# Twenty steps of the weights' conversion in the attention, with a second wx buffer

## The chip, the cores and the metric

One core of a Trainium2 chip runs the whole program. The metric is the device time of one execution in microseconds; three timed runs of the kernel before gave 793.96, 794.51 and 795.60, median 794.51.

The engines are named as in the profile: PE is TensorE (PEld its weight loads), DVE is VectorE, ACT is ScalarE, POOL is GpSimd, SP is SyncE, which issues nearly all DMAs here. Each engine works through its own queue in order.

## The reference

Attention over 2 batches, 8 heads, 768 tokens and 64 dimensions, in which a query sees only the keys of its own cluster, and then two MLPs on the 1536 x 512 result. The weights come as float64.

```python
q_assign = np.argmax(np.einsum('bhsd,hcd->bhsc', q_n, c_n), axis=-1)
k_assign = np.argmax(np.einsum('bhsd,hcd->bhsc', k_n, c_n), axis=-1)
mask = q_assign[:, :, :, None] == k_assign[:, :, None, :]
scores = np.where(mask, scale * np.matmul(q, k.transpose(0, 1, 3, 2)), -1e9)
attn = softmax(scores)
x = (attn @ v).transpose(0, 2, 1, 3).reshape(1536, 512)
h = x @ moe_w_in                    # 512 x 2048
x = (h * np.cos(h)) @ moe_w_out     # 2048 x 512
h = x @ moe2_w_in
g = np.where(h >= 1, h, np.where(h <= -1, 0, (h + 1) ** 2 / 4))
out = g @ moe2_w_out
```

## The kernel before, in words

**Two parts of each number.** Products are made nearly exact by splitting a float32 into a high part hi, rounded to PE's short float32, and the rest lo. A product is then three matmuls: hi by hi, hi by lo, lo by hi (`mm3`, L749 to L751).

**The attention** goes through eight pairs of heads (two batches by four). A pair has four units (two heads by two halves of the queries), a unit six slots, so there are 32 units and 192 slots, 24 to a pair. `run_slot` (L664) emits one slot: the transposes of one key tile of the current unit (L569, the probabilities p of three query tiles), two score matmuls for tiles eight slots ahead (L517, L520), and products with v from slots four to eight of the unit (L594, L599, L600). In even slots come plo of two key tiles (L584, on DVE) and one exponential (L535, on ACT); in odd slots one row maximum (L526, on DVE). ACT copies each transposed tile out of PSUM (L572 or L577, phi), then DVE makes plo of it; the tiles' three PSUM banks (pool `ps_t`) are shared with the preparation. Scores have two buffers; the exponential frees one. The transposes that open a unit need the exponential issued two slots before.

While one pair runs, the next is prepared by `prep_pair`, a generator with one step per slot, started in slots 8, 32, 56, 80, 104 and 128. It transposes q and k (L349), makes th and tl on POOL (L321, L322), copies them into st by DMA (L335), assigns clusters, and in its 22nd step makes the parts of v (vv, L481, L482), loads the next v (L231, L232) and copies the one-hot rows oht by eight DMAs (L312). For the pair that is started in slot 80, this is slot 101.

Slots 18 to 179 lie in a manual schedule: PE, ACT, DVE and POOL keep the order of emission there. SP's queue, and everything outside, is ordered by the planner.

**The weights' conversion.** Each chunk is 128 x 2 x 512 of float64, read as pairs of 32-bit words. `issue_chunk` (L130) loads one into the single buffer wraw; `convert_chunk` (L138) turns it into hi and lo in six steps, between yields: abs (L145, ACT), clip (L147, DVE), shift (L149, DVE), or-low (L152, DVE), then or-high (L155, DVE) with hi (L161, POOL) and the issue of the next load, then lo (L164, DVE). Four chunks make the weights of one quarter: chunks 0 and 1 the first input weights, 2 and 3 the first output weights (moe_w_out). All steps run in one sequence, `weight_steps`; `pump(n)` takes n steps. One step is pumped in each of 16 slots of the attention, at the slot's end (slot % 8 == 5 from 69 to 189): chunks 0 and 1 whole, and chunk 2 up to or-low. In the MLP each output tile pumps one step, and `weight` (L194) pumps whatever is still missing before a weight is used.

**The MLPs** go through two layers, four quarters of the hidden dimension and three blocks of 512 tokens: `hidden` makes four tiles of h and their nonlinearity, `output` four tiles of the partial result y, one block behind. So the first two calls of `hidden` come before the first `output`, which reads chunks 2 and 3. Their hi and lo go into a buffer w_1 that exists only once the attention's pool is given up.

Of the kernel before, what the change touches and what calls it, by code (L numbers as in the profile page):

```python
# [1 line left out]

# [6 lines left out]
F32 = mybir.dt.float32  # L9
F32R = mybir.dt.float32r  # L10
# [8 lines left out]
P = 128  # L19
# [4 lines left out]
HIGH_MIN = 2.0 ** -15  # L24
HIGH_MAX = 122876.0
CHUNK = 6
P_BUFS = 6
NF = 2
NDVE = 2
# [4 lines left out]
def attention_moe_moe(  # L34
# [25 lines left out]
    HS = S // 2  # L60
# [51 lines left out]
    def next_slot():  # L112
        now[0] += 1
        for f, args in due.pop(now[0], ()):
            f(*args)
# [9 lines left out]
    w0pool = ctx.enter_context(tc.tile_pool(name="w0pool", bufs=1))  # L125
    wslot = []
    wchunks = []
    wraw = {}

    def issue_chunk(n):  # L130
        if n >= len(wchunks):
            return
        src, c0, _ = wchunks[n]
        raw = w0pool.tile([P, 2, 512], I64, tag="wraw", bufs=1, name=f"wraw{n}")
        nc.sync.dma_start(raw, src[:, c0:c0 + 2])
        wraw[n] = raw

    def convert_chunk(n):  # L138

        _, c0, w = wchunks[n]  # L140
        words = wraw.pop(n).bitcast(I32).rearrange("p c (f t) -> p c f t", t=2)
        low, high = words[:, :, :, 0], words[:, :, :, 1]
        x = w0pool.tile([P, 2, 512], F32, tag="wx", bufs=1, name=f"wx{n}")
        xi = x.bitcast(I32)
        nc.scalar.activation(x, high.bitcast(F32), AF.Abs)  # L145
        yield
        nc.vector.tensor_scalar(x, x, HIGH_MIN, HIGH_MAX, ALU.max, ALU.min)  # L147
        yield
        nc.vector.tensor_scalar(xi, xi, 3, 0x3FFFFFFF,  # L149
                                ALU.logical_shift_left, ALU.bitwise_and)  # L150
        yield
        nc.vector.scalar_tensor_tensor(xi, low, 29, xi,  # L152
                                       ALU.logical_shift_right, ALU.bitwise_or)
        yield
        nc.vector.scalar_tensor_tensor(xi, high, -0x40000000, xi,  # L155
                                       ALU.bitwise_and, ALU.bitwise_or)
        if not wslot:
            wslot.append(w0pool.tile([P, 2, 4, 512], F32R, tag="w_0", name="w_0"))
        t = wslot[w % 4]
        hi, lo = t[:, 0, c0:c0 + 2], t[:, 1, c0:c0 + 2]  # L160
        nc.gpsimd.tensor_scalar(hi, x, 1.0, 0.0, ALU.mult, ALU.add)  # L161
        issue_chunk(n + 1)
        yield
        nc.vector.tensor_tensor(lo, x, hi.bitcast(F32), ALU.subtract)  # L164
        yield
# [7 lines left out]
                                    (l * NQ + qi) * 2 + s))  # L173

    def weight_steps():
        for n in range(len(wchunks)):
            for _ in convert_chunk(n):
                yield n

    wsteps = weight_steps()  # L180

    def pump(n):

        for _ in range(n):
            at[0] += 1
            next(wsteps, None)
# [3 lines left out]
    def weight(l, qi, s):  # L190
        pump(2 * CHUNK * ((l * NQ + qi) * 2 + s + 1) - at[0])
        t = wslot[((l * NQ + qi) * 2 + s) % len(wslot)]
        return t[:, 0], t[:, 1]


    with ExitStack() as actx:
        ap = actx.enter_context(tc.tile_pool(name="apool", bufs=1))
# [308 lines left out]
        def scores(n, step):  # L506

            i, h, hf = units[n // HJ]
            j = hf * HJ + n % HJ
            qt, kt = prepped[i][1][h]  # L510
            if step == 0:
                ptile[n] = ps_s.tile([P, 2, 512], F32, tag="s", name=f"s{n}")
            s = ptile[n]
            cols = slice(j * P, (j + 1) * P)
            kc = slice(step * HS, (step + 1) * HS)
            with tc.issue_after(last_po[0]) if n == 0 and step == 0 else ExitStack():
                nc.tensor.matmul(s[:, step, :HS], qt[:, 0, cols], kt[:, 0, kc],  # L517
                                 start=True, stop=False)
            rows = D + C if i else D + 2 * C
            nc.tensor.matmul(s[:, step, :HS], qt[:rows, 1, cols], kt[:rows, 1, kc],  # L520
                             start=False, stop=True)

        def row_max(n):
            nm = ap.tile([P, 1], F32, tag="nm", bufs=8, name=f"nm{n}")
            s = ptile[n]
            nc.vector.tensor_reduce(nm, s[:, :, :HS], AX.XY, ALU.max, negate=True)  # L526
            ptile[n] = (s, nm)

        def row_exp(n):
            s, nm = ptile[n]  # L530
            u, jj = divmod(n, HJ)
            if jj == 0:
                dens[u] = ap.tile([P, HJ, 2], F32, tag="den", bufs=4, name=f"den{u}")
            p = ap.tile([P, 2, HS], F32, tag="p", bufs=P_BUFS, name=f"p{n}")
            nc.scalar.activation(p, s[:, :, :HS], AF.Exp, bias=nm,  # L535
                                 accum_out=dens[u][:, jj, 0:1])
            ptile[n] = p
            if jj == HJ - 1:
                later(2, inverse, u)
# [25 lines left out]
        def p_transpose(u, kt):  # L565
            ps = ps_t.tile([P, HS], F32, tag="t", name=f"pt{u}_{kt}")
            for jj in range(HJ):
                p = ptile[u * HJ + jj].rearrange("p a n -> p (a n)")
                nc.tensor.transpose(ps[:, jj * P:(jj + 1) * P], p[:, kt * P:(kt + 1) * P], ident)  # L569
            if kt < NF:  # L570
                pt = ap.tile([P, HS], F32, tag="phi", bufs=6, name=f"p{u}_t{kt}")
                nc.scalar.activation(pt, ps, AF.Copy)  # L572
                pts[(u, kt)] = pt
                return
            hi = ap.tile([P, HS], F32R, tag="phi", bufs=6, name=f"phi{u}_{kt}")
            lo = ap.tile([P, HS], F32R, tag="plo", bufs=5, name=f"plo{u}_{kt}")
            nc.scalar.activation(hi, ps, AF.Copy)  # L577
            pts[(u, kt)] = (hi, lo, ps)

        def p_lo(u, kt):  # L580
            if kt < NF:
                return
            hi, lo, ps = pts[(u, kt)]
            nc.vector.tensor_tensor(lo, ps, hi.bitcast(F32), ALU.subtract)  # L584

        def p_v(u, kt):
            i, h, hf = units[u]
            vv, v32 = prepped[i][0]
            if kt == 0:
                opsum[u] = ps_o.tile([P, HS], F32, tag="o", name=f"o{u}")  # L590
            o = opsum[u]
            if kt < NF:
                rows = slice(kt % 2 * D, (kt % 2 + 1) * D)
                nc.tensor.matmul(o[rows], v32[:, h, kt], pts.pop((u, kt)),  # L594
                                 start=(kt < 2), stop=False)
                return
            hi, lo, _ = pts.pop((u, kt))
            lhs = vv[:, kt - NF, h * P:(h + 1) * P]
            nc.tensor.matmul(o, lhs, hi, start=False, stop=False)  # L599
            nc.tensor.matmul(o, lhs, lo, start=False, stop=(kt == NJ - 1))  # L600
            if kt == NJ - 1:
                later(1, o_parts, u)
# [39 lines left out]


        LEAD, PREP, PREP1 = 8, 16, -8
        PV_AT = (4, 4, 5, 6, 7, 8)
        NSLOT = len(units) * NJ
        PAIR = 4 * NJ
# [10 lines left out]
        for u in range(len(units)):  # L658
            for kt in range(NJ):
                pv_slots.setdefault(u * NJ + PV_AT[kt], []).append((u, kt))  # L660
        preps = []
        prep_at = {(i - 1) * PAIR - PREP: i for i in range(2, len(pairs))}
        prep_at[PREP1] = 1
        def run_slot(slot):  # L664
            g = slot + LEAD
            if slot in prep_at:
                preps.append(prep_pair(prep_at[slot]))
            if 0 <= slot < NSLOT:
                p_transpose(slot // NJ, slot % NJ)
            if 0 <= g < NSLOT:  # L670
                scores(g // 2, g % 2)
            for u, kt in pv_slots.get(slot, ()):
                p_v(u, kt)
            if slot % 2 == 0:
                for s in (slot - 1, slot):
                    if 0 <= s < NSLOT:
                        p_lo(s // NJ, s % NJ)
                if 2 <= g < NSLOT + 2:
                    row_exp(g // 2 - 1)
            next_slot()  # L680
            if slot == 60:
                issue_chunk(0)
            preps[:] = [p for p in preps if next(p, 0) != 0]
            if slot % 2 == 1 and 0 <= g < NSLOT:
                row_max(g // 2)
            if 64 <= slot < 192 and slot % 8 == 5:
                pump(1)


# [2 lines left out]
        for slot in range(-max(LEAD, PREP), FIXED[0]):  # L692
            run_slot(slot)
        with tc.manual_schedule(engines={
                mybir.EngineType.PE, mybir.EngineType.Activation,
                mybir.EngineType.DVE, mybir.EngineType.Pool}):
            for slot in FIXED:
                run_slot(slot)
        for slot in range(FIXED[-1] + 1, NSLOT + PV_AT[-1] - NJ + 1):
            run_slot(slot)  # L700
# [138 lines left out]
```

## Time and profile before

| what | value |
|---|---|
| median of the timed runs | 794.51 us |
| the profiled execution | 794.65 us |
| its span (first to last instruction) | 792.8 us |
| mean granted clock of TensorE | 0.996 |
| attention ends, MLP begins (first L749) | 262.18 us |

Busy time is a sum of durations; PE's matmuls overlap one another, so the distance of starts tells more than the duration of one. An "idle before" of an engine counts only where that engine, or what waits for it, is on the path that sets the end. In the windows, PEclk is the granted clock as a share of 2.4 GHz.

### The profile page before, as it was taken

What the parts mean: (1) busy time and instruction counts of PE and PEld (TensorE: products, weight loads), DVE (VectorE), ACT (ScalarE), POOL (GpSimd) and SP (SyncE); (2) the same over time, 40 slices, a digit from 0 to 9 for tenths busy, and PEclk for the clock granted to TensorE, in tenths of its full rate; (3) what the DMA queues carried; (4) which work ended last, traced back from release to release, by engine and by line L of the source; (5) the groups of instructions that cost most, each with busy time, mean ns of one, the idle gap of its engine ahead of it and who ended that gap; (6) DMA issues with size and microseconds to landing.
All of it is one profiled execution on the core that took longest, in us unless ns stands there. A gap on an engine that the chain in (4) does not pass through costs nothing.

```text
span 792.8 us, 10973 instructions
## 1 busy us (share of the span) xinstructions
PE 779.4 (98%) x3963; PEld 635.9 (80%) x3964; DVE 596.7 (75%) x881; ACT 400.7 (51%) x768; POOL 275.8 (35%) x428
## 2 busy tenths in 40 slices
PE   8999999999999989999999999999999999999998
PEld 5777877878787868888888888888888888888886
DVE  6867877977989587778787878888878888655552
ACT  3788888888898555453334344322434323222220
POOL 4257567578545431221122212342131122111110
PEclk9999999999999999999999999999999999999999
DMA  7764754663420013222131121311121221000012
GB/s 167 172 153 113 176 130 105 144 175 94 106 79 29 26 53 107 79 81 107 54 98 62 58 101 54 107 54 53 58 103 54 90 71 53 1 1 0 22 46 93
DMA packets 48565, 65.94 MB, mean 83 GB/s; under 512 B 28032, under 2 KB 33024, under 8 KB 48512
## 3 DMA queue, kind: packets, MB, share of 16 engines
q1 hardware_dynamic: 48368, 65.22, 28.7%
q8 instruction: 31, 0.51, 0.3%
q14 instruction: 22, 0.18, 0.1%
q10 hardware_dynamic: 144, 0.03, 0.0%
HBM read 43.02 MB, written 3.15 MB: 58 GB/s over the span
## 4 chain that ended last, share of the span: by engine, by line
PE 88%; DVE 5%; ACT 4%; issue 1%; POOL 1%; SPq 1%; DMA 0%; ACTq 0%; POOLq 0%
PE y L751 11%; PE y L749 11%; PE y L750 11%; PE h L751 10%; PE h L749 10%; PE h L750 10%; PE pt L569 8%; PE s L517 4%; PE s L520 3%; PE o L594 2%; PE o L600 2%; PE o L599 2%; ACT p L535 1%; PE ptq L349 1%; DVE nm L526 1%
## 5 line engine op out<-in xcount | busy, mean ns | idle before, releaser
L711 POOL TENSOR_SCALAR gh<-g 128x512 fp32r<-128x512 f32 x96 | 70.9, 739 | 289.2 <-DVE g L742 163.8
L749 PE MATMUL h<-xh,w 128*128 128x512 f32 x384 | 149.5, 389 | 0.0
L751 PE MATMUL h<-xh,w 128*128 128x512 f32 x384 | 149.4, 389 | 0.0
L750 PE MATMUL h<-xl,w 128*128 128x512 f32 x384 | 149.4, 389 | 0.0
L526 DVE TENSOR_REDUCE nm<-s 128x1 f32<-128x768 f32 x96 | 91.4, 953 | 33.3 <-PE s L520 32.6
L569 PE MATMUL pt<-ident,p 128*128 128x128 f32 x576 | 98.2, 279 | 2.6 <-DVE plo L584 1.7
L738 ACT ACTIVATE p<-h,ones 128x512 f32<-128x512 f32 x48 | 33.0, 688 | 132.5 <-DVE m L737 132.1
L569 PEld LDWEIGHTS pt<-ident,p 128*128 128x128 f32 x576 | 68.3, 140 | 31.4 <-DVE nm L526 9.0
L535 ACT ACTIVATE p<-s,nm 128x768 f32<-128x768 f32 x96 | 86.4, 900 | 6.6 <-DVE nm L526 5.7
L715 DVE TENSOR_TENSOR gl<-g,gh 128x512 fp32r<-128x512 f32 x96 | 71.1, 741 | 20.8 <-POOL gh L711 15.0
L750 PEld LDWEIGHTS h<-xl,w 128*128 128x128 f32 x384 | 72.1, 188 | 15.0
L751 PEld LDWEIGHTS h<-xh,w 128*128 128x128 f32 x384 | 72.1, 188 | 15.0
L749 PEld LDWEIGHTS h<-xh,w 128*128 128x128 f32 x384 | 72.1, 188 | 14.9
L517 PE MATMUL s<-st,st 128*128 128x384 f32 x192 | 80.5, 419 | 1.5 <-ACT p L535 1.4
L145 ACT ACTIVATE wx<-wraw 128x1024 f32<-128x1024 f32 x32 | 36.4, 1138 | 88.0 <-DMA wraw<-in_moe_w_in_dram 32.7
L584 DVE TENSOR_TENSOR plo<-pt,phi 128x384 fp32r<-128x384 f32 x128 | 67.9, 549 | 14.1 <-ACT phi L577 13.8
L751 PE MATMUL y<-gh,w 128*128 128x512 f32 x192 | 75.6, 394 | 2.7 <-DVE w L164 2.7
L749 PE MATMUL y<-gh,w 128*128 128x512 f32 x192 | 75.3, 392 | 0.0
L750 PE MATMUL y<-gl,w 128*128 128x512 f32 x192 | 75.2, 392 | 0.0
L751 PE MATMUL y<-w,gl 128*128 128x512 f32 x192 | 74.7, 389 | 0.0
L749 PE MATMUL y<-w,gh 128*128 128x512 f32 x192 | 74.7, 389 | 0.0
L750 PE MATMUL y<-w,gh 128*128 128x512 f32 x192 | 74.7, 389 | 0.0
(132 smaller groups left out, 1530.0 us busy)
## 6 DMA issues: line engine op xcount, KB each, us to landing
wraw<-in_moe_w_in_dram SPq DMA_DIRECT2D x16, 1024.0 KB, 5.1
wraw<-in_moe_w_out_dram SPq DMA_DIRECT2D x16, 1024.0 KB, 4.7
st<-t SPq DMA_DIRECT2D x24, 192.0 KB, 4.2
st<-th SPq DMA_DIRECT2D x9, 384.0 KB, 4.0
st<-tl SPq DMA_DIRECT2D x18, 192.0 KB, 4.0
st<-th SPq DMA_DIRECT2D x18, 192.0 KB, 3.9
nat<-in_q_dram SPq DMA_DIRECT2D x8, 384.0 KB, 3.9
nat<-in_k_dram SPq DMA_DIRECT2D x8, 384.0 KB, 5.1
```

Source lines behind the costliest of these rows:

```text
L145: nc.scalar.activation(x, high.bitcast(F32), AF.Abs)
L517: nc.tensor.matmul(s[:, step, :HS], qt[:, 0, cols], kt[:, 0, kc], start=True, stop=False)
L526: nc.vector.tensor_reduce(nm, s[:, :, :HS], AX.XY, ALU.max, negate=True)
L535: nc.scalar.activation(p, s[:, :, :HS], AF.Exp, bias=nm, accum_out=dens[u][:, jj, 0:1])
L569: nc.tensor.transpose(ps[:, jj * P:(jj + 1) * P], p[:, kt * P:(kt + 1) * P], ident)
L584: nc.vector.tensor_tensor(lo, ps, hi.bitcast(F32), ALU.subtract)
L711: nc.gpsimd.tensor_scalar(hi, g, 1.0, 0.0, ALU.mult, ALU.add)
L715: nc.vector.tensor_tensor(lo, g, hi.bitcast(F32), ALU.subtract)
L738: nc.scalar.activation(r, ph, AF.Relu, bias=mone)
L749: nc.tensor.matmul(o, lh, rh, start=first, stop=False)
L750: nc.tensor.matmul(o, lh, rl, start=False, stop=False)
L751: nc.tensor.matmul(o, ll, rh, start=False, stop=last)
```

## The change

Sixteen slots with a step become twenty: 77, 83, 89, 95, and then every slot from 101 to 175 that ends in 1 or 5. Chunks 0 and 1 are converted whole, as before. Chunks 2 and 3 (EARLY) get other cuts: clip and shift form one step, the load of the next chunk is issued with or-high, and hi is a step of its own. Of chunk 2 four steps are taken, then four of chunk 3; hi and lo of both follow in the MLP. By steps, the slots are:

| chunk | abs | clip | shift | or-low | or-high | lo |
|---|---|---|---|---|---|---|
| 0 | 77 (69) | 83 (77) | 89 (85) | 95 (93) | 101 (101), hi too | 105 (109) |
| 1 | 111 (117) | 115 (125) | 121 (133) | 125 (141) | 131 (149), hi too | 135 (157) |
| 2 | 141 (165) | 145 (173) | with clip (181) | 151 (189) | 155 (MLP) | MLP (MLP) |
| 3 | 161 (MLP) | 165 (MLP) | with clip (MLP) | 171 (MLP) | 175 (MLP) | MLP (MLP) |

In brackets: before. wx gets a second buffer and plo loses one of five.

```diff
@@ -1,4 +1,5 @@
 from contextlib import ExitStack
+from itertools import islice
 
 import concourse.bass as bass
 import concourse.tile as tile
@@ -24,6 +25,7 @@
 HIGH_MIN = 2.0 ** -15
 HIGH_MAX = 122876.0
 CHUNK = 6
+EARLY = (2, 3)
 P_BUFS = 6
 NF = 2
 NDVE = 2
@@ -140,12 +142,13 @@
         _, c0, w = wchunks[n]
         words = wraw.pop(n).bitcast(I32).rearrange("p c (f t) -> p c f t", t=2)
         low, high = words[:, :, :, 0], words[:, :, :, 1]
-        x = w0pool.tile([P, 2, 512], F32, tag="wx", bufs=1, name=f"wx{n}")
+        x = w0pool.tile([P, 2, 512], F32, tag="wx", bufs=2, name=f"wx{n}")
         xi = x.bitcast(I32)
         nc.scalar.activation(x, high.bitcast(F32), AF.Abs)
         yield
         nc.vector.tensor_scalar(x, x, HIGH_MIN, HIGH_MAX, ALU.max, ALU.min)
-        yield
+        if n not in EARLY:
+            yield
         nc.vector.tensor_scalar(xi, xi, 3, 0x3FFFFFFF,
                                 ALU.logical_shift_left, ALU.bitwise_and)
         yield
@@ -154,12 +157,16 @@
         yield
         nc.vector.scalar_tensor_tensor(xi, high, -0x40000000, xi,
                                        ALU.bitwise_and, ALU.bitwise_or)
+        if n in EARLY:
+            issue_chunk(n + 1)
+            yield
         if not wslot:
             wslot.append(w0pool.tile([P, 2, 4, 512], F32R, tag="w_0", name="w_0"))
         t = wslot[w % 4]
         hi, lo = t[:, 0, c0:c0 + 2], t[:, 1, c0:c0 + 2]
         nc.gpsimd.tensor_scalar(hi, x, 1.0, 0.0, ALU.mult, ALU.add)
-        issue_chunk(n + 1)
+        if n not in EARLY:
+            issue_chunk(n + 1)
         yield
         nc.vector.tensor_tensor(lo, x, hi.bitcast(F32), ALU.subtract)
         yield
@@ -173,9 +180,18 @@
                                     (l * NQ + qi) * 2 + s))
 
     def weight_steps():
-        for n in range(len(wchunks)):
-            for _ in convert_chunk(n):
-                yield n
+        n = 0
+        while n < len(wchunks):
+            if n != EARLY[0]:
+                yield from convert_chunk(n)
+                n += 1
+                continue
+
+            both = [convert_chunk(m) for m in EARLY]
+            for count in (4, 2):
+                for steps in both:
+                    yield from islice(steps, count)
+            n += len(EARLY)
 
     wsteps = weight_steps()
 
@@ -573,7 +589,7 @@
                 pts[(u, kt)] = pt
                 return
             hi = ap.tile([P, HS], F32R, tag="phi", bufs=6, name=f"phi{u}_{kt}")
-            lo = ap.tile([P, HS], F32R, tag="plo", bufs=5, name=f"plo{u}_{kt}")
+            lo = ap.tile([P, HS], F32R, tag="plo", bufs=4, name=f"plo{u}_{kt}")
             nc.scalar.activation(hi, ps, AF.Copy)
             pts[(u, kt)] = (hi, lo, ps)
 
@@ -642,6 +658,7 @@
 
 
         LEAD, PREP, PREP1 = 8, 16, -8
+        CONVERT = (77, 83, 89, 95, *(n for n in range(101, 180) if n % 10 in (1, 5)))
         PV_AT = (4, 4, 5, 6, 7, 8)
         NSLOT = len(units) * NJ
         PAIR = 4 * NJ
@@ -683,7 +700,7 @@
             preps[:] = [p for p in preps if next(p, 0) != 0]
             if slot % 2 == 1 and 0 <= g < NSLOT:
                 row_max(g // 2)
-            if 64 <= slot < 192 and slot % 8 == 5:
+            if slot in CONVERT:
                 pump(1)
```

## Rows read from the trace of the kernel before

**Rows 1.** The page, busy time, share of the span and instructions of each engine.

```profile
PE 779.4 (98%) x3963; PEld 635.9 (80%) x3964; DVE 596.7 (75%) x881; ACT 400.7 (51%) x768; POOL 275.8 (35%) x428
```

**Rows 2.** Waits of PE: line waited for, us in total, times, longest.

```profile
PE y L751 <- DVE w L164: 2.7, 1, 2.7
```

**Rows 3.** Timeline of PE, 276 to 300 us: start, us, instruction [idle before <-releaser].

```profile
285.71 0.40 PE L750 MATMUL y<-gl,w 128*128 128x512 f32 x1
288.81 0.79 PE L751 MATMUL y<-gh,w 128*128 128x512 f32 x1 [2.71 <-DVE w L164]
...
291.96 0.41 PE L749 MATMUL y<-gh,w 128*128 128x512 f32 x1
...
299.48 0.39 PE L749 MATMUL h<-xh,w 128*128 128x512 f32 x1
```

**Rows 4.** Windows: PE, PEld, DVE, ACT, POOL busy, PEclk, DMA share, GB/s.

```profile
18.90:25.70 6.80, 5.50 (x40) 5.00 (x39) 6.09 (x10) 4.51 (x10) 1.36 (x3) 1.00 0.51 127
...
288.60:292.00 3.40, 3.19 (x8) 2.51 (x9) 3.23 (x6) 2.70 (x4) 0.62 (x1) 0.50 0.02 6
```

**Rows 5.** Timelines of DVE and of ACT, 243 to 306 us: chunks 2 and 3.

```profile
269.46 1.22 DVE L164 TENSOR_TENSOR w<-wx,w 128x1024 fp32r<-128x1024 f32 x1
...
287.55 1.21 DVE L164 TENSOR_TENSOR w<-wx,w 128x1024 fp32r<-128x1024 f32 x1
...
271.67 1.12 ACT L145 ACTIVATE wx<-wraw 128x1024 f32<-128x1024 f32 x1
```

**Rows 6.** Timeline of PE, first transposes of slots 42, 66, 90, 114 and 138.

```profile
80.22 0.27 PE L569 MATMUL pt<-ident,p 128*128 128x128 f32 x1
...
109.89 0.27 PE L569 MATMUL pt<-ident,p 128*128 128x128 f32 x1
...
140.02 0.27 PE L569 MATMUL pt<-ident,p 128*128 128x128 f32 x1
...
170.89 0.27 PE L569 MATMUL pt<-ident,p 128*128 128x128 f32 x1
...
201.01 0.27 PE L569 MATMUL pt<-ident,p 128*128 128x128 f32 x1
```

**Rows 7.** The chain that ended last, 249 to 262 us: start, us, what.

```profile
251.08 1.11 DVE wx L152
...
253.53 1.13 DVE wx L155
```

**Rows 8.** Instructions on tile wx: ns min/median/max, first and last start us, forms.

```profile
L145 ACT ACTIVATE wx<-wraw x32: 1106/1131/1187, 114.6 to 670.6; 128x1024 f32<-128x1024 f32 x32
L147 DVE TENSOR_SCALAR wx<-wx x32: 684/694/1011, 124.5 to 671.8; 128x1024 f32<-128x1024 f32 x32
...
L155 DVE SCALAR_TENSOR_TENSOR wx<-wraw,wx x32: 1211/1218/1528, 155.0 to 675.0; 128x1024 int32<-128x1024 int32 x32
```

**Rows 9.** Timelines of DVE and of PE, 184 to 212 us: slots 136 and 137.

```profile
199.09 1.01 DVE L584 TENSOR_TENSOR plo<-pt,phi 128x384 fp32r<-128x384 f32 x2
...
199.98 0.49 PE L569 MATMUL pt<-ident,p 128*128 128x128 f32 x3
```

**Rows 10.** Timeline of SP, 75 to 300 us: start, us until the last issue.

```profile
161.02 4.98 SPq L312 DMA_DIRECT2D st<-oht  x8
166.10 0.53 SPq L135 DMA_DIRECT2D wraw<-in_moe_w_in_dram  x1
```

**Rows 11.** Line L135, the loads into wraw, all 32 of them.

```profile
DMA to landing us min/median/max: 4.6/4.9/6.6
```

**Rows 12.** Timeline of ACT, 165 to 177 us: slot 112.

```profile
168.48 0.49 ACT L577 ACTIVATE phi<-pt 128x384 fp32r<-128x384 f32 x1 [0.19 <-PE pt L569]
169.03 0.90 ACT L535 ACTIVATE p<-s,nm 128x768 f32<-128x768 f32 x1
```

**Rows 13.** Timelines of DVE and of POOL, 153 to 168 us: slots 105 to 107.

```profile
159.38 0.96 DVE L526 TENSOR_REDUCE nm<-s 128x1 f32<-128x768 f32 x1 [0.47 <-PE s L520]
...
160.49 1.05 POOL L161 TENSOR_SCALAR w<-wx 128x1024 fp32r<-128x1024 f32 x1
```

## The prediction

> **What bounds the kernel now.** I read the page first: TensorE is busy for 98% of the span [rows 1], so only time in which it stands still, or runs at half rate, can be won. The list of what it waits for comes next. It has one large entry: 2.7 us, once, for the last step of a weight's conversion, L164 [rows 2]. The timeline of PE around it shows where [rows 3]: in the first output tile, at 285.94 us (285.71 plus one start distance), PE should have issued the third product of a group, and issued it at 288.81. The reader should then see that it is slow afterwards: from 288.81 to 291.96 there are seven starts in 3.15 us, while the 33 starts after that take 7.52, or 0.228 each. The windows give the reason: the granted clock is 0.50 between 288.6 and 292.0, the 1.2 GHz level [rows 4]. ACT and DVE tell why chunk 3 was late [rows 5]: its first step (L145) starts at 271.67, after chunk 2's last (269.46 plus 1.22), as both use the one wx buffer, and its own last ends only at 288.76.
>
> After that PE has no wait until the end. So what the change can win in the MLP is this stall; everything else lies in the attention. There I read the start of a slot from its first transpose: the preparation of the next pair repeats every 24 slots, so starts 24 slots apart show what the steps between them cost [rows 6]. From slot 42 to 66, without steps, the period is 29.67 us. With abs, clip and shift in it, it is 30.13; with or-low, or-high, hi and lo 30.87; with abs, clip and shift of chunk 1 30.12.
>
> **The parts, one by one.**
>
> 1. The stall in the first output goes: 288.81 - 285.94 = 2.87 us of standing, and 3.15 - 7 x 0.228 = 1.55 of half rate. Sum **-4.4**. Chunks 2 and 3 keep only hi and lo there: two of about 1.05 on POOL and two of about 1.21 on DVE, 4.5 us in all, emitted in the first four tiles after 262 and wanted at 285.94. Nothing later in the MLP is priced: all steps come four earlier, beside a PE that doesn't wait. If that cover were gone, each late step would cost up to its 1.2 us.
>
> 2. The sixteen old steps go from their places. In the three periods they cost 0.46, 1.20 and 0.45. I read 0.46 as the price of an abs (1.13 on ACT, ahead of an exponential that PE soon needs), clip and shift as free, and 1.20 for three steps of 1.22 on DVE. Over both kinds, 6.4 us of DVE work cost 1.2, or 0.19 per us. The seven steps after slot 138 (one abs, 5.0 us of DVE) come to 0.46 + 0.95 by these prices. Sum -2.11 - 1.41 = **-3.5**.
>
> 3. In the attention's tail, or-low and or-high of chunk 2 lie on the chain that ended last, 1.11 and 1.13 long [rows 7]. The gain is between 0 and 2.2; I take half, as PE's own work there is nearly dense: **-1.1**.
>
> 4. The new steps. Clip and shift four times (0.69 each) and or-low and or-high four times (1.22 each, [rows 8]) are 15.3 us of DVE; at 0.19 per us **+2.9**. Lo of chunk 1, now in slot 135, is taken apart: the two plo it pushes start at 199.09 and take 1.01, so the first ends at about 199.6, and PE's transposes at 199.98, three tiles on, need its bank [rows 9]. Slack 0.4, so 1.22 - 0.4 = **+0.8**. Abs of chunk 2 falls in slot 141, the same place in a period as 69 and 117: **+0.5**. Abs of chunk 0 moves to slot 77, where nothing like it is seen: between 0.46 and the whole 1.13, I take **+0.8**, nearer the middle as neither end is closer.
>
> 5. Chunk 1's abs is the term that decides. It moves from slot 117 to slot 111, but its load can't move. The issue follows or-high in slot 101, as now, and SP issues in order: eight copies of oht from 161.02 to 166.0, then the load at 166.10 [rows 10]. It lands 4.9 us later [rows 11], at 171.0. Abs would be due on ACT just before the copy at 168.48 [rows 12]. Being in order, ACT stands; then abs to 172.1, that copy (0.55 to the next start), and the exponential (0.90) to 173.6. The transposes of slot 114, which read it, began at 170.89 [rows 6]: 2.7 late, 2.8 with a hand-over. Inside this lies lo of chunk 0, moved from slot 109 to 105. DVE gets to it at 160.3 (159.38 plus a row maximum of 0.96), but POOL ends hi only at 161.54 [rows 13]; with its own 1.22 it holds back the plo pair behind it by 2.5 us, and PE, which waits for their banks, by an estimated 1.1. The load doesn't move with PE, so the later wait shrinks by that, and the two together stay at **+2.8**. Bounds: 0.7 (abs 0.46, lo 0.23, no wait) to 4.4 (with the clock, below).
>
> 6. Chunk 3's load is issued after or-high in slot 155, and its abs is in slot 161. Step and load take 1.22 + 4.9, or 6.1 us, of six slots that are 7.4 us in a period with preparation and shorter where none runs. Wait between 0 and 0.9, I take 0.4; with abs **+0.9**.
>
> 7. Edits at nothing: the second wx buffer only takes a wait away; plo with four buffers is reused by the same kt one unit (six slots) later, while its last reader comes three slots after it. The loads of chunks 2 to 4 go into SP's queue in slots 131, 155 and 175, at 0.4 to 0.5 each, and hi of chunk 1 into POOL's in slot 131 (1.05); behind them stand the copies, th and tl of the last pair, wanted from slot 160 on. If that cover were gone, a held copy would cost PE up to the load's own wait for DVE.
>
> Sum: -4.4 - 3.5 - 1.1 + 2.9 + 0.8 + 0.5 + 0.8 + 2.8 + 0.9 = **-0.3 us**. It is made against the profiled execution (794.65, span 792.8), which lies 0.14 above the median of the three runs, 794.51; the forecast for the median is 794.2.
>
> A rule that speaks against the change: the Trainium skill (SBUF — State Buffer, Who interferes with whom) says that a DVE instruction with two SBUF inputs and a GpSimd instruction that reads SBUF lock each other out for a whole instruction. The row shows or-high at 1.21 at best and 1.53 at worst [rows 8], a stretch of 0.3, less than the 1.05 of POOL's hi [rows 13]. By the rule at its worst the ten such steps would add 1.05 each to DVE, some 2 us at 0.19 per us; the sum goes by the row.
>
> **Rivals.**
>
> Faster: the two load waits don't bite, because SP gets the loads out ahead of the copies of oht, or because earlier stalls have made PE late enough. Then 2.8 falls to 0.7 and 0.9 to 0.5: 2.5 less, **791.7**. For it: the load needs only or-high of its own slot, so its place behind the copies is the planner's choice, which a shifted plan may change. Against: in this very slot the load stands behind the eight copies [rows 10].
>
> Slower: DVE has no room for 20 steps in 99 slots, after 16 in 121, and its work there is dearer than 0.19 per us. It decides from 0.32 on (0.13 more on 15.3 us is 2.0). At twice the price, 0.38, **797.1**. For it: without the free clip and shift the price was 0.33 already (1.20 for 3.66), two steps are now doubled to 1.38, and most stand four or six slots apart instead of eight. Against: 0.19 is what was measured over places that differ.
>
> Beside it, within the range: PE stands for about 1.6 us before slot 114. In a stretch with a wait of 1.2 the clock stayed at 1.00, after one of 2.7 it was 0.50 [rows 4]; if it falls, up to 1.6 more, 795.8.
>
> The change doesn't do what it says: hi and lo of chunk 3 still come too late, and the stall stays. Then 798.6; against it, 24 us from 262 to 286 for 4.5 us of work.
>
> **How the numbers follow.** About 0.2% (1.6 us) is what a measurement of this kernel can tell from no change. The forecast, within that, has 0.43; the faster rival 0.30; the slower 0.24; the stall that stays 0.03. So faster 0.30, same 0.43, slower 0.27. The likeliest case alone reaches from 793.0 to 796.0. The range goes down to the faster rival with a tail worth 1.5, 791.3, and up to the slower rival with 0.4 for the second load's bound, 797.5.
>
> **What would show it.** PE's list of waits without L164 under L751, and a clock of 1.00 in the MLP; no conversion rows between slot 180 and the MLP. In the attention: ACT L145 waiting for the DMA of wraw in slot 111, for 1 to 3 us, and the period from slot 90 to 114 some 3 us longer than 30.87; DVE L164 waiting for POOL in slot 105. If ACT doesn't wait there, point 5 is wrong and the kernel is faster; if the periods without such a wait grow by over 1.5 us each, the price of DVE work is wrong and it is slower.

## The result, and the profile after

The kernel is **slower**: median 802.19 us against 794.24 for the kernel before on the same chip, ratio 1.0097 (95% interval 1.0072 to 1.0122). The forecast was 794.2 with a range up to 797.5. The profiled execution took 799.8, with a span of 797.7, so it lies below its median; a repetition (below) gave one of 801.5. In the kernel after, abs, clip, shift, or-low, or-high, hi and lo are lines L147, L149, L152, L155, L158, L167 and L171, the transposes L585, plo L600, and mm3 L766 to L768.

First the page's busy time, which answers to [rows 1], and PE's list of waits, which answers to [rows 2] (line waited for, us in total, times, longest).

```profile
PE 780.7 (98%) x3964; PEld 634.5 (80%) x3964; DVE 600.0 (75%) x881; ACT 400.5 (50%) x768; POOL 276.5 (35%) x428
```

```profile
PE pt L585 <- DVE plo L600: 4.4, 8, 1.4
PE s L533 <- ACT p L551: 2.1, 3, 1.2
...
PE ptq L365 <- DVE plo L600: 1.0, 1, 1.0
PE h L766 <- ACT p L755: 0.9, 2, 0.8
PE y L766 <- DVE acc L805: 0.9, 1, 0.9
PE h L766 <- DVE g L745: 0.5, 1, 0.5
```

The one large entry of before, PE's wait for the last step of chunk 3, is gone. In its place stand many small ones, in the attention (pt, ptq) and in the MLP (h, y). The timeline of PE gives the first transposes of slots 42, 66, 90, 114 and 138, which answer to [rows 6].

```profile
79.92 0.49 PE L585 MATMUL pt<-ident,p 128*128 128x128 f32 x3
...
109.59 0.49 PE L585 MATMUL pt<-ident,p 128*128 128x128 f32 x3
...
140.06 0.49 PE L585 MATMUL pt<-ident,p 128*128 128x128 f32 x3
...
173.36 0.61 PE L585 MATMUL pt<-ident,p 128*128 128x128 f32 x3 [1.42 <-DVE plo L600]
...
204.32 0.49 PE L585 MATMUL pt<-ident,p 128*128 128x128 f32 x3
```

The periods are 29.67, 30.47, **33.30** and 30.96 us (before 29.67, 30.13, 30.87 and 30.12). The third holds the two waits that point 5 named. Here they are in the timelines of SP, ACT, DVE and PE; they answer to [rows 10, 12, 13].

```profile
160.65 4.98 SPq L328 DMA_DIRECT2D st<-oht  x8
165.73 0.53 SPq L137 DMA_DIRECT2D wraw<-in_moe_w_in_dram  x1
...
171.21 1.12 ACT L147 ACTIVATE wx<-wraw 128x1024 f32<-128x1024 f32 x1 [1.97 <-DMA wraw<-in_moe_w_in_dram]
172.24 0.48 ACT L593 ACTIVATE phi<-pt 128x384 fp32r<-128x384 f32 x1
...
161.20 1.51 DVE L171 TENSOR_TENSOR w<-wx,w 128x1024 fp32r<-128x1024 f32 x1 [1.15 <-POOL w L167]
...
163.23 0.55 PE L365 MATMUL ptq<-ident,nat 128*128 128x128 f32 x3 [0.97 <-DVE plo L600]
```

The load again stands behind eight copies of oht, abs stands 1.97 us on ACT for it, and the copy phi behind abs comes at 172.24; lo of chunk 0 stands 1.15 for POOL. PE stands 0.97 and 1.42. The profile puts the second of these waits to plo, whose phi is the copy behind abs; the exponential that point 5 named follows that copy on ACT. Over slots 18 to 180 the attention takes 205.12 us (before 199.18); the MLP begins at 267.33 instead of 262.18.

Now the MLP, in windows (as [rows 4]: us, then PE, PEld, DVE, ACT, POOL busy, PEclk, DMA share, GB/s), each placed alike against the MLP's start: first before, then after.

```profile
262.00:294.00 32.00, 29.29 (x124) 23.71 (x123) 23.91 (x33) 18.05 (x29) 13.89 (x17) 0.95 0.10 34
...
545.00:571.00 26.00, 26.00 (x116) 21.55 (x115) 21.75 (x29) 9.32 (x14) 7.24 (x10) 1.00 0.22 79
```

```profile
267.00:299.00 32.00, 31.54 (x140) 25.47 (x139) 24.26 (x34) 18.69 (x31) 14.16 (x17) 1.00 0.10 34
...
550.00:576.00 26.00, 24.02 (x102) 18.55 (x102) 21.91 (x28) 6.82 (x10) 8.57 (x11) 1.00 0.25 81
```

The counts of matmuls are what to read. In the first 32 us there are 16 more than before, 3.6 us at 0.228 each, and the granted clock is 1.00: the stall went, less a small loss of 0.9. But in 26 us about the change of layers there are **14 fewer**, some 3.2 us, where PE had never waited. The timelines of POOL, DVE and PE show what stands there. In them acc holds the running sums of y; xh and xl are the high and low parts of the next layer's input x, made of acc, as gh and gl are those of the nonlinearity's result g.

```profile
519.22 2.50 POOL L167 TENSOR_SCALAR w<-wx 128x1024 fp32r<-128x1024 f32 x2
...
556.42 2.50 POOL L167 TENSOR_SCALAR w<-wx 128x1024 fp32r<-128x1024 f32 x2
560.67 1.53 POOL L728 TENSOR_SCALAR xh<-acc 128x512 fp32r<-128x512 f32 x1 [1.75 <-DVE acc L805]
...
556.49 1.52 DVE L732 TENSOR_TENSOR xl<-acc,xh 128x512 fp32r<-128x512 f32 x1 [0.74 <-POOL xh L728]
557.93 2.06 DVE L171 TENSOR_TENSOR w<-wx,w 128x1024 fp32r<-128x1024 f32 x1
559.92 0.68 DVE L805 TENSOR_TENSOR acc<-y,acc 128x512 f32<-128x512 f32 x1
560.52 1.21 DVE L171 TENSOR_TENSOR w<-wx,w 128x1024 fp32r<-128x1024 f32 x1
...
560.65 0.50 PE L766 MATMUL y<-w,gh 128*128 128x512 f32 x1 [0.92 <-DVE acc L805]
564.46 0.47 PE L766 MATMUL h<-xh,w 128*128 128x512 f32 x1 [0.77 <-ACT p L755]
```

Two chunks were ready at once, in the two wx buffers. POOL makes both hi's side by side, DVE one lo at 2.06 (alone 1.21) ahead of the last sums acc, and the other ahead of their low parts. PE waits for acc to free a bank, and later for the nonlinearity. At 519 the same pair cost nothing in this execution; in the repetition it cost 1.5. So such a pair does not cost in every place and execution.

### The profile page after: what moved, and what is told of

It is laid out like the page before. It is cut to its first block, busy times and chain, and to the rows that moved or that the text cites. A ratio compares the mean times of both kernels' runs of the same rounds, so it can differ in the third digit from the quotient of the medians.

```text
span 797.7 us, 10978 instructions
## 1 busy us (share of the span) xinstructions
PE 780.7 (98%) x3964; PEld 634.5 (80%) x3964; DVE 600.0 (75%) x881; ACT 400.5 (50%) x768; POOL 276.5 (35%) x428
## 4 chain that ended last, share of the span: by engine, by line
PE 52%; DVE 25%; DMA 7%; POOL 6%; ACT 5%; issue 4%; SPq 1%; POOLq 0%; ACTq 0%; DVEq 0%
PE pt L585 7%; PE y L768 5%; PE y L766 5%; PE y L767 5%; PE h L766 4%; PE h L768 4%; PE h L767 4%; DVE gl L732 4%; POOL gh L728 4%; PE s L533 3%; PE s L536 3%; DMA wraw<-in_moe_w_in_dram 3%; DVE g L745 3%; DMA wraw<-in_moe_w_out_dram 3%; DVE wx L155 3%
## 5 line engine op out<-in xcount | busy, mean ns | idle before, releaser
L728 POOL TENSOR_SCALAR gh<-g 128x512 fp32r<-128x512 f32 x96 | 68.2, 711 | 322.8 <-DVE g L759 172.4
L766 PE MATMUL h<-xh,w 128*128 128x512 f32 x384 | 150.1, 391 | 1.5 <-ACT p L755 0.9
L768 PE MATMUL h<-xh,w 128*128 128x512 f32 x384 | 149.4, 389 | 0.0
L585 PE MATMUL pt<-ident,p 128*128 128x128 f32 x576 | 98.1, 279 | 4.9 <-DVE plo L600 4.4
L585 PEld LDWEIGHTS pt<-ident,p 128*128 128x128 f32 x576 | 68.2, 140 | 34.1 <-DVE plo L600 8.2
L732 DVE TENSOR_TENSOR gl<-g,gh 128x512 fp32r<-128x512 f32 x96 | 74.1, 773 | 20.3 <-POOL gh L728 13.4
L766 PEld LDWEIGHTS h<-xh,w 128*128 128x128 f32 x384 | 72.1, 188 | 18.4 <-DVE g L745 1.3
L768 PEld LDWEIGHTS h<-xh,w 128*128 128x128 f32 x384 | 72.1, 188 | 15.1
L147 ACT ACTIVATE wx<-wraw 128x1024 f32<-128x1024 f32 x32 | 36.4, 1138 | 95.0 <-DMA wraw<-in_moe_w_in_dram 36.9
L600 DVE TENSOR_TENSOR plo<-pt,phi 128x384 fp32r<-128x384 f32 x128 | 67.8, 549 | 15.5 <-ACT phi L593 15.1
L766 PE MATMUL y<-w,gh 128*128 128x512 f32 x192 | 74.8, 390 | 0.9 <-DVE acc L805 0.9
L768 PE MATMUL y<-w,gl 128*128 128x512 f32 x192 | 74.7, 389 | 0.0
L768 PE MATMUL y<-gh,w 128*128 128x512 f32 x192 | 74.7, 389 | 0.0
L766 PE MATMUL y<-gh,w 128*128 128x512 f32 x192 | 74.7, 389 | 0.0
```

Of the source, the lines that this page charges most:

```text
L728: nc.gpsimd.tensor_scalar(hi, g, 1.0, 0.0, ALU.mult, ALU.add)
L732: nc.vector.tensor_tensor(lo, g, hi.bitcast(F32), ALU.subtract)
L766: nc.tensor.matmul(o, lh, rh, start=first, stop=False)
L768: nc.tensor.matmul(o, ll, rh, start=False, stop=last)
```

## Experiments

Times are medians, each with the ratio (and its 95% interval) to the kernel before, timed beside it. "Tile" is twelve matmuls of h or y, counted from the MLP's start; a tile's loss is its distance to the next less 12 x 0.2267 us. Such a loss need not be a wait: other products can stand inside a tile.

### What the MLP loses

**e1_after_again**, the changed kernel as it is.

> The changed kernel once more, for a second trace: its four times spread from 799.8 to 803.9 us, and the trace is of the fastest. Theory A (the loss is fixed in place: some 5 us in the attention, 3 at the change of layers): the same two losses, and what the slower executions have more is another wait at the change of layers or in the MLP. Rival B (the spread is one load that lands sooner or later): the wait for the DMA in slot 111 differs by 1 us or more between the two traces. Median 800 to 803.

Measured: 801.90, 1.0093 (1.0080 to 1.0106). The attention is the same within 0.2 us; the MLP's losses sum to 5.5 us (4.5 before, 3.9 in the first profile): 0.9 at tiles 3 and 4, 1.5 at 93 to 95, 3.1 at 106 to 110. So the slow part beyond the attention lies at two places in the MLP.

**e2_phase**: the steps fall on the same MLP tiles as in the kernel before.

```diff
-            pump(1)
+            if (l, qi, blk) != (0, 0, 1):
+                pump(1)
```

> The four steps that the MLP is ahead are given back: no step is pumped in the second call of hidden, so from the first output on every tile has the step that it has in the kernel before; attention and buffers as changed. Theory A (what is lost at the change of layers, 3.2 us, comes from where the steps fall among the tiles): PE starts lose nothing there, 3 us less than the changed kernel, about 796.5 to 799. Rival B (it comes from the second wx buffer, which lets abs, clip and shift of the next chunk go ahead of the layer's own work): the loss stays, 800 to 803.

Measured: 801.61, 1.0093 (1.0079 to 1.0106), with the losses at the same tiles. The four steps' lead is not the cause.

**e3_own_wx**: chunk 3 alone has the second buffer.

```diff
-        x = w0pool.tile([P, 2, 512], F32, tag="wx", bufs=2, name=f"wx{n}")
+        x = w0pool.tile([P, 2, 512], F32, tag="wx3" if n == 3 else "wx", bufs=1, name=f"wx{n}")
```

> The second buffer is given to chunk 3 alone; all other chunks share one wx as before, and the steps lie as changed. Theory A (place of the steps): the loss of 3 us at the change of layers stays, 800 to 803. Rival B (second buffer): it goes, 796.5 to 799. Besides, abs of chunk 1 must now wait for lo of chunk 0, which is over by then: no difference in the attention.

Measured: **797.58**, 1.0044 (1.0030 to 1.0057), 4.3 us below e1, timed beside it; attention as in e1, the MLP's losses 1.8. So the second buffer for the later chunks carries 4.3 us.

**e4_before_wx2**: the kernel before, with two wx and four plo buffers.

> The kernel before with the two buffer counts of the change alone (wx two, plo four), all steps at their old places. Theory A: with the second buffer the planner can begin chunk 3 while chunk 2 waits for its parts, so that the stall of 4.4 us in the first output shrinks or goes and nothing else moves: 789.5 to 792.5. Rival B (the second buffer costs at the change of layers): the stall goes and 3 us come back there, 792.5 to 795. If the buffers do nothing alone: 794.

Measured: 793.01, 0.9983 (0.9973 to 0.9993). The stall goes (-4.4), 2.8 comes back at tiles 0 and 3, and nothing is lost at 93 to 110. So two buffers need not lose there. What differs is the planner's order. Below is the order on POOL in these kernels and in three that follow, from hi of chunk 18 on: W is a hi, a dot is one gh or xh. The pairs to compare are the second (chunks 20 and 21) and the third (22 and 23).

```
after, e1, e2  WW..........WW.............WW.......WW
e3             WW..........W.....W........W..W.....W..W
e4, e13        WW.........W.....W........W.W.......WW (e13: W..W)
e5             WW..........W.....W........W..W.....WW
e14            WW.........W.W............W.W.......WW
```

Only the kernels that lose at tiles 93 to 107 have the hi's of chunks 20 and 21, and of 22 and 23, side by side. Chunks 18 and 19 stand side by side in all of these and cost nothing.

**e5_one_buf_20_23**: two buffers for all but these four chunks.

```diff
-        x = w0pool.tile([P, 2, 512], F32, tag="wx", bufs=2, name=f"wx{n}")
+        tag = "wx3" if n % 2 and n not in range(20, 24) else "wx"
+        x = w0pool.tile([P, 2, 512], F32, tag=tag, bufs=1, name=f"wx{n}")
```

> The changed kernel, with two wx buffers for all chunks but 20 to 23, which share one: the four that are converted about 485 to 565 us, where the changed kernel loses time and the kernel with a second buffer for chunk 3 alone doesn't. Theory A (with two buffers both chunks of a part are ready together, their two hi's stand back to back on POOL and their two lo's behind them on DVE; where such a pair falls on the change of layers, the sums acc and their parts come late for the next products): the losses at the output tiles about 521 and 557 us go, time 797.6, between 796.6 and 798.6. Rival B (two buffers cost time throughout the MLP, by SBUF or port traffic of abs and hi running early): most of the loss stays, 800.5 to 802.5.

Measured: 798.59, 1.0053 (1.0041 to 1.0065), the upper edge of theory A. Tiles 93 to 109 lose nothing, 110 loses 0.9; but the next pair, chunks 24 and 25, now costs 1.6 at tiles 117 and 118. The windows show it: 112 matmuls about the change of layers, and 82 instead of 90 behind it.

```profile
550.00:576.00 26.00, 25.30 (x112) 20.60 (x111) 21.78 (x29) 9.30 (x14) 6.74 (x9) 1.00 0.21 75
580.00:600.00 20.00, 18.86 (x82) 14.97 (x81) 14.76 (x19) 9.30 (x14) 6.68 (x6) 1.00 0.25 91
```

That pair is there in the changed kernel too and costs it nothing; why it does here is open.

**e13_two_buf_20_23**: the complement; e3 with `n in (3, 21, 23)` for `n == 3`.

> The kernel with a second buffer for chunk 3 alone (797.6), and a second one for chunks 20 to 23 too: the complement of the run in which only these four shared one. In this kernel's order on POOL the hi's of 20 and 21 stand six gh or xh apart, those of 22 and 23 with one between them; in the changed kernel both stand side by side. Theory A (the two hi's side by side and the two lo's behind them cost, not the second buffer as such): no wait about 521 us and at most 0.9 about 557, time 797.6 (796.6 to 798.6). Rival B (a second buffer in use there costs by itself): 801 to 802.

Measured: 796.59, 1.0025 (1.0014 to 1.0037), the lower edge of theory A. The windows of the same stretches show no loss beside e3 (25.50 busy, 113 matmuls).

```profile
515.00:533.00 18.00, 18.00 (x82) 14.89 (x81) 17.00 (x23) 4.66 (x8) 9.08 (x8) 1.00 0.17 56
550.00:576.00 26.00, 25.78 (x113) 20.70 (x112) 21.96 (x27) 9.48 (x15) 9.42 (x9) 1.00 0.23 77
```

A second buffer in use there costs nothing. Of the kernels run, those lose whose two hi's and two lo's come in one go where DVE owes the sums.

### What the attention loses

The first three kernels here are e3 with another list of slots; the fourth is the changed kernel with the list of the third.

**e7_lo0_later**: lo of chunk 0 in slot 109 instead of 105.

```diff
-        CONVERT = (77, 83, 89, 95, *(n for n in range(101, 180) if n % 10 in (1, 5)))
+        CONVERT = (77, 83, 89, 95, 101, 109, *(n for n in range(111, 180) if n % 10 in (1, 5)))
```

> As the run before, but only lo of chunk 0 moves, from slot 105 to 109; abs of chunk 1 stays in slot 111 and with it the wait for its load. If the wait for POOL's hi and the wait for the load cost about the same (1.0 and 1.4 us of idle time on PE in the changed kernel): slots 102 to 108 get 1 to 1.4 us shorter, slots 108 to 114 stay at 9.7 or grow by the lo step (0.2 to 0.5), time 796.5 to 797.2. If the load's wait alone counts: 797.6, no change. If POOL's alone: 795.5.

Measured: 799.26, 1.0059 (1.0043 to 1.0075), outside all three. Slots 102 to 108 get 1.3 shorter (9.40 to 8.07), and then more than that is lost: slots 108 to 114 take 11.03 (9.56 in e3). ACT, PE and the windows:

```profile
172.52 1.12 ACT L147 ACTIVATE wx<-wraw 128x1024 f32<-128x1024 f32 x1 [3.38 <-DMA wraw<-in_moe_w_in_dram]
...
174.66 0.90 PE L585 MATMUL pt<-ident,p 128*128 128x128 f32 x3 [2.74 <-DVE plo L600]
```

```profile
172.00:174.60 2.60, 0.00 (x0) 0.00 (x0) 0.55 (x2) 2.08 (x3) 0.00 (x0) 0.99 1.16 293
174.60:178.00 3.40, 3.33 (x13) 3.24 (x14) 1.86 (x5) 2.47 (x7) 0.55 (x2) 0.51 1.03 233
```

The load lands when it did, so abs waits 3.38 instead of 1.86 (e3), PE stands 2.74, and its clock falls to the 1.2 GHz level for 3.4 us, which it didn't do in the changed kernel: slots 114 to 120 take 8.28 instead of 6.94. The two waits are one: it ends with the load.

**e6_lo0_abs1_later**: abs of chunk 1 in slot 117 as well, the rest one place later.

> A second wx buffer for chunk 3 alone (797.6 with the changed kernel's slots), and lo of chunk 0 moved from slot 105 to 109, abs of chunk 1 from 111 to 117, the rest one place later, the last step in slot 179. Theory A (point 5 of the prediction: in slot 105 lo waits for POOL's hi, in 111 abs waits for its load; 2.8 us together): the period of slots 90 to 114 falls from 33.2 to about 31 us, time 795.5 (794.8 to 796.5). Rival B (the waits are only symptoms; DVE's extra work in these slots costs the same wherever it lies): the period falls but others rise as much, time 797 to 798.5.

Measured: 797.93, 1.0047 (1.0033 to 1.0061), which by the time alone would be rival B. The trace says otherwise. The period of slots 90 to 114 is 30.47 (33.26 in e3), 2.8 less, as theory A has it. But abs of chunk 3 now comes in slot 165, four slots behind the issue of its load, and the same thing happens there: ACT stands 1.9 us for it, PE 2.24, the clock falls, and slots 168 to 174 take 12.0 us instead of 7.7.

```profile
237.76 1.12 ACT L147 ACTIVATE wx<-wraw 128x1024 f32<-128x1024 f32 x1 [1.91 <-DMA wraw<-in_moe_w_out_dram]
...
240.19 0.33 PE L585 MATMUL pt<-ident,p 128*128 128x128 f32 x1 [2.24 <-ACT p L551]
```

**e9_spaced**: every abs at least ten slots behind its load's issue.

```diff
-        CONVERT = (77, 83, 89, 95, *(n for n in range(101, 180) if n % 10 in (1, 5)))
+        CONVERT = (77, 83, 89, 95, 101, 109, 117, 121, 125, 131, 135, 139, 145, 149, 151, 155, 165, 169, 173, 177)
```

> Twenty steps by slot 177, a second wx buffer for chunk 3 alone, and every abs at least ten slots behind the issue of its load (chunk 1: 101 to 117, chunk 2: 135 to 145, chunk 3: 155 to 165), lo of chunk 0 in slot 109. Theory A (what is lost in the attention beyond DVE's own price is the wait of an abs for its load, with PE's clock falling where the wait is long): period of slots 90 to 114 about 30.5, no unit of six slots above 9.1, slots 18 to 180 in about 202 us (205.1 in the changed kernel), MLP begins near 263.5; time 794.3 (793.3 to 795.8). Rival B (twenty steps cost the same wherever they lie): slots 18 to 180 stay at 204.5 to 205.5, time 797 to 798.

Measured: **793.66**, 0.9991 (0.9982 to 1.0001), no different from before, with twenty steps in the attention. PE's waits from 60 to 256 us are short:

```profile
PE pt L585 <- DVE plo L600: 2.8, 4, 0.9
PE s L533 <- ACT p L551: 0.7, 1, 0.7
PE pt L585 <- ACT p L551: 0.5, 2, 0.3
```

The period of slots 90 to 114 is 30.47, slots 18 to 180 take 203.18 (205.27 in e3). The first product of the MLP comes at 260.94, earlier than theory A has it, but the attention's last products stand behind it, and the next product of its tile comes at 264.54:

```profile
260.94 0.48 PE L766 MATMUL h<-xh,w 128*128 128x512 f32 x1
261.37 0.87 PE L610 MATMUL o<-p_t,v 128*64 128x384 f32 x4
...
264.54 0.49 PE L767 MATMUL h<-xl,w 128*128 128x512 f32 x1
```

PE doesn't stand there. The second tile begins at 267.18, 1 us later than theory A has it, and 14.3 us after slot 180 (14.8 in e3). So lo's wait for POOL and abs's wait for its load were together worth 2.8 us in that period. Against e3, each beside its own runs of before, the median falls by 3.9. Between the two traces it is 3.0: 2.1 less in slots 18 to 180 (other periods grow there), 0.5 from slot 180 to the second tile, and 0.7 at tile 110, which no longer loses; the start is 0.2 later.

**e14_spaced_wx2**: e9 with the changed kernel's two buffers for all chunks.

> The run with every abs ten slots behind its load (793.7), and two wx buffers for all chunks, as in the changed kernel; its order on POOL has the hi's of 20 and 21 one xh apart and those of 22 and 23 too, no longer side by side, and pairs side by side only from chunk 24 on. Theory A: losses at the change of layers of at most 1 us, time 793.7 to 795.2. Rival B (a second buffer costs 4.3 us in the MLP whatever the order): 797 to 798.5.

Measured: 794.45, 1.0004 (0.9993 to 1.0015). The change as it was made, with other slots only, is as fast as before: its order on POOL no longer has the two pairs side by side, and tiles 109 and 110 lose 0.8.

### Is there something faster?

**e8_old_slots_own**: e3 with the sixteen old slots.

> The sixteen old slots, with the new cuts (chunk 2 through or-high in slot 189, chunk 3 in the MLP's first four tiles) and a buffer of its own for chunk 3 alone. If the four more steps in the attention are what the changed kernel pays for and one buffer for all later chunks avoids the loss at the change of layers: attention as before (slots 18 to 180 in 199.2 us), the stall in the first output gone (-4.4), some 2 us given back where the two lo's stand ahead of the first nonlinearities: 792 (790.5 to 793.5). Rival (the planner puts the rest of chunk 2 and chunk 3 on the path between attention and MLP, so that the MLP begins later): 794 to 796.

Measured: 796.93, 1.0035 (1.0023 to 1.0048), above both. The first product of the MLP comes early (258.4), but, as in e9, products of the attention stand inside the first tile, and the second begins 15.3 us after slot 180, as before: nothing is won or lost there. Tiles 3 and 4 lose 5.8, more than the stall that went, with PE standing 3.87 for the first nonlinearities and the clock at the lower level after it. On DVE the planner had put chunk 3's steps between the two last xt of the attention, and both lo's ahead of the nonlinearity.

**e10_before_own**: the kernel before with a buffer of its own for chunk 3 (e3's line) and four plo buffers.

> The kernel before with its sixteen slots and old cuts, a buffer of its own for chunk 3 and four plo buffers: the second buffer's gain alone, without a second buffer for the later chunks. Attention as before; the stall of the first output (3.9 and 0.6) goes; about 2.8 us are given back in the MLP's first four tiles, where both lo's stand ahead of the first nonlinearity on DVE, as in the run with two buffers for all chunks (2.3 and 0.5): 793.0 (792.2 to 794). If the second buffer for later chunks were what made that run faster: 794.2 or more.

Measured: **792.21**, 0.9979 (0.9969 to 0.9988): the lowest ratio of all, 1.9 us below before; its interval overlaps that of e4 (0.9973 to 0.9993), so the two can't be told apart. The stall goes, 2.8 comes back at tiles 0 and 3, as forecast. The latter is the last fault in the MLP, in the timelines of PE and DVE:

```profile
274.93 0.50 PE L749 MATMUL h<-xh,w 128*128 128x512 f32 x1 [2.13 <-DVE g L728]
...
271.77 2.51 DVE L164 TENSOR_TENSOR w<-wx,w 128x1024 fp32r<-128x1024 f32 x2
```

**e11_before_own_manual**: e10, with DVE in the order of emission in the first four hidden tiles.

```diff
-                g = hidden(l, qi, blk)
+                if (l, qi, blk) == (0, 0, 0):
+                    with tc.manual_schedule(engines={mybir.EngineType.DVE}):
+                        g = hidden(l, qi, blk)
+                else:
+                    g = hidden(l, qi, blk)
```

> As the run before, and DVE keeps the order of emission in the MLP's first four hidden tiles, so that each lo stands behind a nonlinearity. Theory A (the order on DVE is what costs in the MLP's first tiles): the 2.8 us of the first four tiles go too, and the stall stays away if chunk 3's lo still comes before the first output (about 285 us): 790.3 (789.5 to 792). Rival B (chunk 3's steps, now one by one in the MLP, come late again): the stall returns in part, 792 to 794.5.

Measured: 795.04, 1.0009 (0.9996 to 1.0022), no different from before and above both ranges; the mechanism is that of rival B. The trace is of an execution of 792.94, so what the slower ones lose beyond it is not shown. In it, tiles 0 and 3 lose nothing (5 and 6 lose 0.8), but chunk 3 is late again and PE waits for its hi.

```profile
289.98 0.50 PE L749 MATMUL y<-gh,w 128*128 128x512 f32 x1 [2.44 <-POOL w L161]
```

**e12_spaced_manual**: e9 with the same edit.

> The run with every abs ten slots behind its load, and DVE in the order of emission in the MLP's first four hidden tiles. Theory A: the losses at tiles 3 to 5 (0.66, 0.29 and 0.17 in the kernel with a buffer for chunk 3 alone) go, 1.1 us below the same kernel without this: 793.2 (792 to 794.8). Rival B (DVE is simply full there, whatever the order): no difference from it.

Measured: 793.50, 0.9996 (0.9985 to 1.0007), not to be told from e9, as rival B has it. In the trace the losses at tiles 3 to 6 fall from 1.3 to 0.7.

## Why the prediction was wrong

The repetition's profile (801.5) is nearest to the median, so the working is held against it: slots 18 to 180 +5.8, from there to the MLP -0.5, the MLP +1.5, start -0.2; +6.6 in all.

- **Point 1: the step that failed.** The stall went in full, -4.4 (tiles 8 and 9), with the clock at 1.00, and chunks 2 and 3 had left the path between attention and MLP. But "Nothing later in the MLP is priced: all steps come four earlier, beside a PE that doesn't wait", and point 7's "the second wx buffer only takes a wait away", were wrong together: 0.9 at tiles 3 and 4 and 4.6 at tiles 93 to 110 came instead. The later steps did change places, not by the lead of four (e2), but because with two buffers the planner could gather two chunks and run their hi's and lo's in one go. Why it did so with these slots is open. That PE waits for nothing says nothing of DVE, which at the change of layers had 21.75 busy of 26 us before. This is 5.9 of the 6.9 us by which the sum missed, the MLP at +1.5 where -4.4 stood.
- **Points 2, 4, 5, 6 together** gave +5.2 for the attention; +5.8 was measured. In point 2 only six of the "seven steps" make up its 5.0 us; the seventh, or-low in slot 189, is the one that point 3 counts. Point 5 held in mechanism: the load behind eight copies, ACT's wait of 1.97 within the 1 to 3 forecast, lo's wait for POOL. In size it was near: the period grew by 2.4 where some 3 were forecast, and e6 and e9 took 2.8 away. That this is its sum to the tenth is partly luck, as they moved abs and the waits out of the period but not lo's own work, which the 2.8 of the point includes (0.2). PE's second wait ended with plo, not with the exponential that the point names; both hang on the same abs. Its remark that the two waits share one total is what e7 showed.
- **Point 6:** no wait; six slots were just enough (the load issued at 228.39, abs at 233.15). At four slots it cost over 4 us (e6).
- **Point 4:** twenty steps without waits (e9) take 203.18; less what remains without steps by point 2, 199.18 - 3.5 = 195.7, that is 7.5, where the working has 6.2 (8.7 less the waits, 2.1 and 0.4). If all of the 1.3 is put down to DVE's price on its 15.3 us, that is 0.27 per us instead of 0.19: dearer, but below the 0.32 from which the slower rival decides.
- **Point 3:** -1.1 forecast, -0.5 measured.
- **Point 7's** four plo buffers cost nothing: with them e10 takes 199.18 for slots 18 to 180, as before.
- **The rivals.** SP didn't get the load out early, the stall didn't stay, and before slot 114 the clock didn't fall. The slower rival has the sign right and the cause wrong: periods without a wait grew by 0.3, 0.8 and, from slot 138 to 162, 1.2, below the 1.5 that it named.

By runs: of e1's 7.7 us, 4.3 go with the second buffer of the later chunks (e1 to e3) and 3.9 with the other list of slots (e3 to e9). Of these 3.9 the two waits are shown as 2.8, in one period. What is left, -0.5, holds the four more steps' price against the stall. What is not settled is why the planner gathers chunks 20 to 23 with the changed kernel's slots and not with those of e4 or e14.

## What to carry to other kernels

A second buffer is more than a wait removed: it lets a planner change the order of everything that follows, so compare the order of the engines over the whole program, and look where an engine that nobody waits for now is nearly full. When a step moves ahead, count the distance from its load's issue to its first reader, and every instruction in order behind that reader. Of two waits in a row that end with the same event, removing the first gains nothing.

## What was not expected of the hardware

A DVE lo took 2.06 us beside the pair of hi's on POOL and 1.21 alone, and the xl in front of it 1.52 where it else takes 0.69; the two hi's took 2.50 where one alone takes 1.05. In the rows read for the prediction, or-high was stretched by 0.3 only. The Trainium skill (SBUF — State Buffer, Who interferes with whom) says that a DVE instruction with two SBUF inputs and a GpSimd one that reads SBUF shut each other out; the trace agrees here, with 0.85 more for the lo. The prediction quoted this and put it at nothing by the row of or-high in the attention; in the MLP it is part of what such a pair takes from DVE. It doesn't cost by itself: in e13 the hi of chunk 23 took 2.02, and the tiles there lost no more than in e3.

The clock's fall doesn't follow the length of PE's last wait alone. In e6 PE stood 2.24 us, and the clock fell; in e11 it stood 2.44, and the clock stayed at 1.00. The windows behind each, e6 first:

```profile
240.20:243.80 3.60, 3.60 (x14) 3.41 (x15) 1.72 (x3) 2.18 (x5) 0.55 (x2) 0.53 0.00 0
```

```profile
288.60:292.20 3.60, 2.22 (x10) 1.84 (x11) 3.60 (x6) 1.27 (x2) 1.91 (x2) 1.00 0.72 225
```
